# One chained attention–mixer–FNet kernel on Trainium2: thinner widening behind the last projection, slots opened inside channel block 0, slabs copied from SBUF

## The chip, the cores and the metric

The kernel runs on one core of a Trainium2 chip. The metric is the device time of one execution in microseconds. Of the kernel before three runs are shown; their median is 944.74 us, and they lie between 943.64 and 945.34.

## The reference: what is computed

Three layers follow one another on an activation of 4 × 576 tokens by 512 channels.

```python
def attention(q, k, v, omega):                    # 4 x 8 heads x 576 x 64, 128 features
    def phi(x):
        h = einsum('bhsd,md->bhsm', x, omega) - sum(x * x, -1) / 2
        return exp(h - max(h, -1)) / sqrt(m)
    q_p, k_p = phi(q * scale), phi(k * scale)
    kv, z = einsum('bhsm,bhsd->bhmd', k_p, v), sum(k_p, 2)
    return einsum('bhsm,bhmd->bhsd', q_p, kv) / (einsum('bhsm,bhm->bhs', q_p, z) + 1e-06)

def mixer(x, w_tok1, w_tok2, w_ch1, w_ch2):       # 576 -> 256 -> 576, 512 -> 1536 -> 512
    u = x + (relu(x.T @ w_tok1) @ w_tok2).T
    return u + relu(u @ w_ch1) @ w_ch2

def fourier(x, w_ch1, w_ch2):                     # 512 -> 2048 -> 512
    u = x + real(fft(fft(x, axis=1), axis=2))
    un = (u - mean(u)) / sqrt(var(u) + 1e-06)
    return u + relu(un @ w_ch1) @ w_ch2
```

The activations are float32; the weights of the two MLPs arrive as 64-bit floats.

## The kernel before

**Products.** Every operand of a product is split into a high and a low part of float32, and a product is three products on TensorE (PE): high by high, low by high, high by low. A channel MLP step takes one of twelve weight slabs (128 hidden units of `w_ch1` and `w_ch2`, high and low, 1 MB): `up` (L777) makes 12 matmuls into an H bank of PSUM, `relu` takes the high part on ACT (`hh`, L864) and the low part on DVE (`hl`, L865), and `down` (L902) makes 12 matmuls into four A banks that collect over all twelve slabs. `mlp` (L868) writes them in this order: up(i), relu(i), down(i−1), then a piece of other work. The tokens are cut into five blocks of 512 (the last has 256), in the order 0, 4, 1, 2, 3; every second block takes the slabs in reverse order.

**Widening.** The 64-bit weights are turned into pairs of float32 on the core (`widen`, L325 to L375), a chunk of 128 × 1024 words at a time. A chunk is loaded into `stg`, goes through seven DVE steps (take L342, rest L353, size L357, high L361, low L365, unit L369, scaled L373; ACT scales once in between), and its result in `cvo` is stored to DRAM as `kept` by `store` (L407 for a slab). There are two buffers each of `stg`, `cvy` and `cvo`, used in turn, so chunk i+2 writes its `cvo` where chunk i's was. `weave` (L384) strings the steps of neighbouring chunks together: four chunks of the token weights, the twelve slabs 0 to 11, then sixteen chunks for the last layer, which the prediction counts on from 12. `Side` (L200) gives them out: each slot of the attention and each step of an MLP adds an allowance in us to a credit, and steps are issued while the credit covers their cost. The allowances are a row of constants (L37):

```python
SLOT0_US, SLOT1_US, SLOT_US, FIRST_US, SHORT_US, CH_US, FF_US, S_US, SAVED_US = 1.2, 0.45, 1.2, 3.9, 1.2, 4.3, 3.8, 1.6, 4.6
side.step(0.0 if n < 6 else SLOT0_US if n < 10 else SLOT1_US if n < 36 else SLOT_US)
```

**Slots.** `Slots` (L258) keeps slabs in SBUF. `refill` goes through the sequence of slabs to come; for the first that isn't there it takes a free slot, or the one whose slab is needed latest, and fetches the slab from `kept` on SP's queue (`fetch`, L733). It stops at a slab that has not been stored yet. Two slots (`wa`) are there from the last projection on, three (`wb`) from attention's end, and five more (`wc`, `wd`) from the end of channel block 0. From attention's end on the widening's loads and stores go by POOL's queue (`side.queue`), fetches stay on SP's. A slot holds 1 MB.

**Attention's end.** `attention()` runs over slots n; the projections end at slot `n_all`, and seven slots follow in which the last `numer` (L583), `divide` (DVE L596, L599), transposes (`turn_x`, L617) and the first `up` of channel block 0 are written. The token mixing of the last quarter of the tokens (`tok_mix`) is cut into pieces in the list `fill`: two `hid` (L668) and eight `back` (six matmuls at L681, then a DVE add into `x2` at L684). A piece is taken per slot, and in channel block 0 one per step; what is left is written ahead of the last step's split. Token products take their bank by `bank`: while the list `spare` is not empty, they go around its banks (A, A, H), otherwise they have two S banks of their own. `spare` is emptied after attention.

**Tables.** `tables()` (L943, L944) loads two tables for the Fourier transform, by SP's and POOL's queues, ahead of the second channel block; `dft` first reads them in the fourth.

Of the kernel before, what the change touches and what calls it, by code (L numbers as in the profile page):

```python
# [28 lines left out]
NWB = 3  # L29
IDLE = 16  # L30
# [6 lines left out]
SLOT0_US, SLOT1_US, SLOT_US, FIRST_US, SHORT_US, CH_US, FF_US, S_US, SAVED_US = 1.2, 0.45, 1.2, 3.9, 1.2, 4.3, 3.8, 1.6, 4.6  # L37
# [220 lines left out]
class Slots:  # L258
# [3 lines left out]
    def __init__(self, seq, fetch, ready, wait):  # L262
        self.seq, self.fetch, self.ready, self.wait = seq, fetch, ready, wait
        self.free, self.here, self.at = [], {}, 0
        self.allow = lambda q, slot: True

    def refill(self, need=None):
        for q in range(self.at, len(self.seq)):
# [35 lines left out]
def mix_kernel(ctx: ExitStack, tc: tile.TileContext, qt, kt, va, om, w1, w2, wch, wff, t1, t2, out):  # L304
# [96 lines left out]
    kept = {}  # L401
    whole = set()

    def slab(j):
        def store(st, free):
            kept[j] = dram.tile([128, 2, 1024], F32, name="kept")
            side.queue.dma_start(out=kept[j], in_=st["o"].bitcast(F32))  # L407
            whole.add(j)
            free()
# [323 lines left out]
    def fetch(x, pl_, tag):  # L733
# [3 lines left out]
        else:  # L737
            t = pl_.tile([128, 2, 1024], F32R, tag=tag, name="w")
            sync.dma_start(out=t.bitcast(F32), in_=kept[x])
        return t  # L740

    def wait_whole(x):
# [5 lines left out]
                fetch, lambda x: x in whole, wait_whole)  # L748
    mix.allow = lambda q, slot: q < len(mix.seq) - 2 or slot[1] in ("wa0", "wa1", "wd")
# [32 lines left out]
    def attention():  # L782
# [35 lines left out]
        for n in range(-1, n_all + LAG_X):  # L818
            while loads and at[loads[0]] <= n + AHEAD_LOAD:
                load(*loads.pop(0))  # L820
            if n == n_all:
                enter_mlp()
            if 0 <= n < n_all:
# [8 lines left out]
            if n >= 2:  # L832

                side.step(0.0 if n < 6 else SLOT0_US if n < 10 else SLOT1_US if n < 36 else SLOT_US)
# [19 lines left out]
    side.defer, side.queue = 0, pool  # L854

# [12 lines left out]
    def mlp(steps, first_of, u, cols, down, budget, prepare, twice=False):  # L868
# [3 lines left out]
        for i, x in enumerate(steps):  # L872
# [11 lines left out]
            if not last:  # L884
                if fill:
                    fill.pop(0)()
# [5 lines left out]
    def ch_block(at_, c, u, prepare, budget):  # L892
# [12 lines left out]
        mlp(turns(NCH, at_), ch_first, u, cols, down, budget, prepare)  # L905
# [7 lines left out]
    def mixed():  # L913
        while fill:
            fill.pop(0)()

    ch_block(0, 0, u, [lambda: (mixed(), ch_split(BLOCKS[1], u2))], FIRST_US)
    u = u2
    pt.close()
    xu = ctx.enter_context(tc.tile_pool(name="xu", bufs=1, side="right", reuse_waits="tile"))  # L920
    c2 = ctx.enter_context(tc.tile_pool(name="c2", bufs=1, side="right", reuse_waits="tile"))

    pw = ExitStack()
    wc = pw.enter_context(tc.tile_pool(name="wc", bufs=1, side="right", reuse_waits="tile"))
    mix.free.extend((wc, f"wc{i}") for i in range(4))
# [676 lines left out]
```

## Time and profile before

| | |
|---|---|
| median of three runs | 944.74 us (943.64 to 945.34) |
| the profiled execution, its own time | 942.83 us |
| its span in the profile | 940.6 us |
| granted TensorE clock | 1.00 |
| PE busy | 930.3 us, 99% |
| DVE busy | 633.4 us, 67% |
| ACT, POOL busy | 305.7 and 118.9 us |
| DMA | 216.5 MB, mean 230 GB/s |
| chain that ended last | PE 92%, DVE 5%, DMA 1%, ACT 1% |

Between the profiled execution's time and its span lie 2.2 us around the program. The engines run side by side; a busy share near 100% names the engine that sets the time, and the idle time before its instructions, with what released each, says what could still be won. The chain that ended last is followed back from the last instruction; it lies on PE nearly throughout.

### The profile page before, as it was taken

The numbers are of one execution on the slowest core, as the hardware profiler recorded it, in microseconds if no ns is written. First come the engines' busy times: TensorE is split into PE (matmuls) and PEld (weight loads), VectorE is DVE, ScalarE is ACT, GpSimd is POOL, SyncE is SP. The second block draws the span as 40 slices with busy tenths as digits, with TensorE's granted clock in tenths as the row PEclk, the third lists the DMA queues.
The fourth block names the chain that finished last, engine by engine and source line by source line (L and its number), as shares of the span: only waits on it lengthen the run. The fifth ranks groups of instructions, "written<-read, shape, count | busy, mean of one in ns | idle before, by whom it ended". The sixth has DMA issues, their size and how long they took to land.

```text
span 940.6 us, 14116 instructions
## 1 busy us (share of the span) xinstructions
PE 930.3 (99%) x5360; PEld 830.1 (88%) x5360; DVE 633.4 (67%) x1259; ACT 305.7 (32%) x709; POOL 118.9 (13%) x110
## 2 busy tenths in 40 slices
PE   9999999989999999999999999999999999999998
PEld 8999999978889888888888888889999998899986
DVE  5987999896775778777853667766565457533342
ACT  5986777722121322122121122222311113211121
POOL 3453444221211122011000000000000000000000
PEclk9999999999999999999999999999999999999999
DMA  8765554687897586573245368739766656687764
GB/s 275 237 212 183 182 214 153 257 301 286 327 419 306 201 319 220 187 277 126 90 175 195 124 207 267 240 106 400 257 232 230 221 191 230 231 263 251 247 214 153
DMA packets 68258, 216.48 MB, mean 230 GB/s; under 512 B 5600, under 2 KB 14432, under 8 KB 54240
## 3 DMA queue, kind: packets, MB, share of 16 engines
q1 hardware_dynamic: 60992, 172.40, 52.5%
q0 software_dynamic: 7056, 43.06, 12.4%
q8 instruction: 43, 0.70, 0.3%
q14 instruction: 23, 0.19, 0.1%
q10 hardware_dynamic: 144, 0.13, 0.0%
HBM read 169.30 MB, written 42.47 MB: 225 GB/s over the span
## 4 chain that ended last, share of the span: by engine, by line
PE 92%; DVE 5%; DMA 1%; ACT 1%; issue 0%; POOL 0%; DVEq 0%; SPq 0%; ACTq 0%
PE H L777 23%; PE A L902 16%; PE A L1474 14%; PE H L1461 12%; PE A L1268 7%; PE A L507 4%; PE N L583 3%; PE H L541 2%; PE A L668 1%; PE A L566 1%; PE S L1081 1%; PE S L1094 1%; PE S L681 1%; PE H L668 1%; PE A L681 1%; PE S L668 1%
## 5 line engine op out<-in xcount | busy, mean ns | idle before, releaser
L777 PE MATMUL H<-uh,w 128*128 128x512 f32 (+1 forms) x800 | 215.2, 354 | 2.1 <-DVE x L684 2.1
L777 PEld LDWEIGHTS H<-uh,w 128*128 128x128 f32 x800 | 136.4, 189 | 22.3 <-DVE x L684 2.3
L864 ACT ACTIVATE hh<-H 128x512 fp32r<-128x512 f32 (+1 forms) x92 | 49.0, 533 | 270.4 <-PE H L777 270.2
L777 PE MATMUL H<-ul,w 128*128 128x512 f32 (+1 forms) x304 | 113.5, 373 | 0.4 <-DVE ul L764 0.4
L902 PE MATMUL A<-hh,w 128*128 128x512 f32 (+1 forms) x480 | 108.7, 369 | 0.0
L865 DVE SCALAR_TENSOR_TENSOR hl<-H,hh 128x512 fp32r<-128x512 f32 (+1 forms) x92 | 55.7, 606 | 65.5 <-ACT hh L864 65.3
L1474 PE MATMUL A<-w2t,b 128*128 128x512 f32 x384 | 99.2, 394 | 0.0
L902 PEld LDWEIGHTS A<-hh,w 128*128 128x128 f32 x480 | 84.2, 188 | 15.0
L1461 PE MATMUL H<-b,w1t 128*128 128x384 f32 x480 | 91.5, 336 | 0.0
L1461 PEld LDWEIGHTS H<-b,w1t 128*128 128x128 f32 x480 | 85.0, 188 | 4.0 <-DVE tmp L1505 0.3
L1474 PEld LDWEIGHTS A<-w2t,b 128*128 128x128 f32 x384 | 70.6, 188 | 11.8
L525 ACT ACTIVATE f<-A,mx 128x128 f32<-128x128 f32 x240 | 69.5, 396 | 22.9 <-DVE mx L521 22.5
L777 PEld LDWEIGHTS H<-ul,w 128*128 128x128 f32 x304 | 57.3, 189 | 9.9 <-DVE ul L764 0.8
L902 PE MATMUL A<-hl,w 128*128 128x512 f32 (+1 forms) x240 | 59.2, 368 | 0.0
L1268 PE MATMUL A<-w,hh 128*128 128x512 f32 x192 | 50.5, 395 | 0.0
L902 PEld LDWEIGHTS A<-hl,w 128*128 128x128 f32 x240 | 42.6, 188 | 7.6
L521 DVE TENSOR_REDUCE mx<-A 128x4 f32<-128x512 f32 x70 | 47.4, 680 | 1.7 <-PE A L507 1.4
L541 PE MATMUL H<-v,f 128*128 128x65 f32 x320 | 40.1, 270 | 0.5 <-ACT f L525 0.4
L1466 ACT ACTIVATE b<-tmp 128x384 fp32r<-128x384 f32 x16 | 8.4, 525 | 98.1 <-DVE tmp L1527 98.1
L361 DVE SCALAR_TENSOR_TENSOR cvo<-cvy,cvo 128x1024 int32<-128x1024 int32 (+2 forms) x32 | 39.7, 1240 | 0.5
L1268 PEld LDWEIGHTS A<-w,hh 128*128 128x128 f32 x192 | 34.6, 189 | 6.1
L541 PEld LDWEIGHTS H<-v,f 128*128 128x128 f32 x320 | 38.9, 191 | 0.9 <-ACT f L525 0.7
(263 smaller groups left out, 1687.5 us busy)
## 6 DMA issues: line engine op xcount, KB each, us to landing
w<-kept SPq DMA_DIRECT2D x60, 1024.0 KB, 6.9
w2t<-kept SPq DMA_DIRECT2D x55, 512.0 KB, 4.9
w1t<-kept SPq DMA_DIRECT2D x48, 512.0 KB, 5.1
stg<-in_wff_dram POOLq DMA_DIRECT2D x16, 1024.0 KB, 6.6
kept<-cvo POOLq DMA_DIRECT2D x13, 1024.0 KB, 7.2
stg<-in_wch_dram SPq DMA_DIRECT2D x9, 1024.0 KB, 6.2
kept<-cvo POOLq DMA_DIRECT2D x16, 512.0 KB, 7.4
kept<-so SPq DMA_DIRECT2D x16, 512.0 KB, 8.0
```

The source lines that it names most:

```text
L361: dve.scalar_tensor_tensor(out=st["h"], in0=st["y"].bitcast(I32), scalar=-0x80000000, in1=st["h"], op0=ALU.bitwise_and, op1=ALU.bitwise_or)
L507: pe.matmul(out=pj[:, p_ * 256:p_ * 256 + 256], lhsT=a[:, c, :], rhs=w, start=(n == 0), stop=(n == 2), skip_group_check=True)
L521: dve.tensor_reduce(out=mx, in_=p4, axis=AX.X, op=ALU.max, negate=True)
L525: act.activation(out=f[:, hh], in_=p4[:, hh], func=AF.Exp, bias=mx[:, hh])
L541: pe.matmul(out=kvp[b, g][:, hh * 65:hh * 65 + 65], lhsT=ft["k", i, g][:, hh, :], rhs=src["v", i, int(off > 0)][:, 4 * g + hh, :], start=( ...
L777: pe.matmul(out=hb[:, 0:n], lhsT=w(a, kk), rhs=u[:, kk, 0:n], start=(c == 0), stop=(c == 11))
L864: act.activation(out=hh, in_=hb[:, 0:n], func=AF.Relu)
L865: dve.scalar_tensor_tensor(out=hl, in0=hb[:, 0:n], scalar=0.0, in1=hh, op0=ALU.max, op1=ALU.subtract)
L902: pe.matmul(out=acc[i][:, 0:cols], lhsT=a[:, cs], rhs=v, start=(n == 0 and c_ == 0), stop=(n == NCH - 1 and c_ == 2))
L1268: pe.matmul(out=acc[t], lhsT=a[:, t * 128:t * 128 + 128], rhs=w, start=(n == 0 and c_ == 0), stop=(n == NFF - 1 and c_ == 2))
L1461: pe.matmul(out=to, lhsT=w[:, a, cs], rhs=v[:, q], start=(start and n == 0), stop=(n == 5), skip_group_check=True)
L1474: pe.matmul(out=acc[t], lhsT=h[n // 2][:, t * 128:t * 128 + 128], rhs=w[:, n % 2], start=(begins and n == 0), stop=(ends and n == 2))
```

## The change

Seven edits, in the order of the diff:

- `LOOK`: `refill` looks six slabs ahead of the step at work, not to the end of the sequence.
- `FIRST_US`, the widening's allowance a step in channel block 0, goes from 3.9 to 4.4.
- *Copies* (`direct`): from attention's end on, when a slab's widening is done, it is first offered to `refill`; if that takes it, it is copied from `cvo` to its slot in SBUF on POOL's queue, and the store to `kept` is issued behind the copy.
- `spare` is emptied when the last projection's slots begin (`n == n_all`).
- The seven slots behind the last projection get an allowance of 0.45 (`SLOT1_US`) and no longer 1.2.
- In channel block 0 two pieces of `fill` are written per step; as soon as the list is empty, the token mixing's tiles are given up and the five slots `wc` and `wd` opened (`filled`), which was done behind the block.
- `tables()` is called ahead of the third channel block and no longer ahead of the second.

```diff
@@ -27,6 +27,7 @@
 BLK = 512
 
 NWB = 3
+LOOK = 6
 IDLE = 16
 NBLK = (NTOK + BLK - 1) // BLK
 
@@ -34,7 +35,7 @@
 
 
 
-SLOT0_US, SLOT1_US, SLOT_US, FIRST_US, SHORT_US, CH_US, FF_US, S_US, SAVED_US = 1.2, 0.45, 1.2, 3.9, 1.2, 4.3, 3.8, 1.6, 4.6
+SLOT0_US, SLOT1_US, SLOT_US, FIRST_US, SHORT_US, CH_US, FF_US, S_US, SAVED_US = 1.2, 0.45, 1.2, 4.4, 1.2, 4.3, 3.8, 1.6, 4.6
 
 
 NP = NFF // 2
@@ -261,11 +262,11 @@
 
     def __init__(self, seq, fetch, ready, wait):
         self.seq, self.fetch, self.ready, self.wait = seq, fetch, ready, wait
-        self.free, self.here, self.at = [], {}, 0
+        self.free, self.here, self.at, self.ahead = [], {}, 0, len(seq)
         self.allow = lambda q, slot: True
 
     def refill(self, need=None):
-        for q in range(self.at, len(self.seq)):
+        for q in range(self.at, min(self.at + self.ahead, len(self.seq))):
             s = self.seq[q]
             if s in self.here:
                 continue
@@ -398,12 +399,17 @@
         return items
 
 
-    kept = {}
+    kept, fresh = {}, {}
     whole = set()
 
     def slab(j):
         def store(st, free):
             kept[j] = dram.tile([128, 2, 1024], F32, name="kept")
+            if mlp0.get("direct"):
+                fresh[j] = st["o"]
+                whole.add(j)
+                mix.refill()
+                del fresh[j]
             side.queue.dma_start(out=kept[j], in_=st["o"].bitcast(F32))
             whole.add(j)
             free()
@@ -736,7 +742,10 @@
             sync.dma_start(out=t.bitcast(F32), in_=kept[x][:, 0:4])
         else:
             t = pl_.tile([128, 2, 1024], F32R, tag=tag, name="w")
-            sync.dma_start(out=t.bitcast(F32), in_=kept[x])
+            if x in fresh:
+                side.queue.dma_start(out=t.bitcast(F32), in_=fresh[x].bitcast(F32))
+            else:
+                sync.dma_start(out=t.bitcast(F32), in_=kept[x])
         return t
 
     def wait_whole(x):
@@ -746,6 +755,7 @@
     mix = Slots([j for c in range(NBLK) for j in turns(NCH, c)]
                 + [(k, p_) for c in range(len(PLAIN)) for p_ in turns(NP, c) for k in (1, 2)],
                 fetch, lambda x: x in whole, wait_whole)
+    mix.ahead = LOOK
     mix.allow = lambda q, slot: q < len(mix.seq) - 2 or slot[1] in ("wa0", "wa1", "wd")
 
     def halves(t, h):
@@ -820,6 +830,7 @@
                 load(*loads.pop(0))
             if n == n_all:
                 enter_mlp()
+                spare.clear()
             if 0 <= n < n_all:
                 project(*order[n])
             sums(n)
@@ -831,7 +842,7 @@
             results(n)
             if n >= 2:
 
-                side.step(0.0 if n < 6 else SLOT0_US if n < 10 else SLOT1_US if n < 36 else SLOT_US)
+                side.step(0.0 if n < 6 else SLOT0_US if n < 10 else SLOT1_US if n < 36 or n >= n_all else SLOT_US)
             if fill and (len(fill) > 3 or n % 2 == 0):
                 fill.pop(0)()
             for fn in early[:3]:
@@ -852,6 +863,7 @@
     pools["S"] = ctx.enter_context(tc.tile_pool(name="ps_s", bufs=2, space=PSUM, reuse_waits="tile")), 2
 
     side.defer, side.queue = 0, pool
+    mlp0["direct"] = True
 
 
     hp = pm.enter_context(tc.tile_pool(name="hp", bufs=2, reuse_waits="tile"))
@@ -865,7 +877,7 @@
         dve.scalar_tensor_tensor(out=hl, in0=hb[:, 0:n], scalar=0.0, in1=hh, op0=ALU.max, op1=ALU.subtract)
         return hh, hl
 
-    def mlp(steps, first_of, u, cols, down, budget, prepare, twice=False):
+    def mlp(steps, first_of, u, cols, down, budget, prepare, twice=False, filled=None):
 
 
         prev = None
@@ -882,14 +894,18 @@
                 down(*prev)
             prev = i, x, h
             if not last:
-                if fill:
-                    fill.pop(0)()
+                for fn in fill[:2]:
+                    fn()
+                del fill[:2]
+                if filled and not fill:
+                    filled()
+                    filled = None
                 side.step(budget / 2 if twice else budget)
         for fn in prepare[1:]:
             fn()
         down(*prev)
 
-    def ch_block(at_, c, u, prepare, budget):
+    def ch_block(at_, c, u, prepare, budget, filled=None):
         acc = [bank("A") for _ in range(4)]
         cols = ch_cols(c)
 
@@ -902,7 +918,7 @@
                     pe.matmul(out=acc[i][:, 0:cols], lhsT=a[:, cs], rhs=v, start=(n == 0 and c_ == 0),
                               stop=(n == NCH - 1 and c_ == 2))
             mix.used()
-        mlp(turns(NCH, at_), ch_first, u, cols, down, budget, prepare)
+        mlp(turns(NCH, at_), ch_first, u, cols, down, budget, prepare, filled=filled)
         for i in range(4):
             for off, n, b, s in pieces(c * BLK, cols):
                 dve.tensor_tensor(out=x2[b][:, i, s:s + n], in0=acc[i][:, off:off + n], in1=x2[b][:, i, s:s + n],
@@ -910,21 +926,20 @@
 
     u = mlp0["u"]
     u2 = operand()
-    def mixed():
-        while fill:
-            fill.pop(0)()
-
-    ch_block(0, 0, u, [lambda: (mixed(), ch_split(BLOCKS[1], u2))], FIRST_US)
+    rooms = {}
+
+    def filled():
+        pt.close()
+        rooms["xu"] = ctx.enter_context(tc.tile_pool(name="xu", bufs=1, side="right", reuse_waits="tile"))
+        rooms["c2"] = ctx.enter_context(tc.tile_pool(name="c2", bufs=1, side="right", reuse_waits="tile"))
+        rooms["wc"] = pw.enter_context(tc.tile_pool(name="wc", bufs=1, side="right", reuse_waits="tile"))
+        mix.free.extend((rooms["wc"], f"wc{i}") for i in range(4))
+        mix.free.append((pm.enter_context(tc.tile_pool(name="wd", bufs=1, reuse_waits="tile")), "wd"))
+
+    pw = ExitStack()
+    ch_block(0, 0, u, [lambda: ch_split(BLOCKS[1], u2)], FIRST_US, filled)
     u = u2
-    pt.close()
-    xu = ctx.enter_context(tc.tile_pool(name="xu", bufs=1, side="right", reuse_waits="tile"))
-    c2 = ctx.enter_context(tc.tile_pool(name="c2", bufs=1, side="right", reuse_waits="tile"))
-
-    pw = ExitStack()
-    wc = pw.enter_context(tc.tile_pool(name="wc", bufs=1, side="right", reuse_waits="tile"))
-    mix.free.extend((wc, f"wc{i}") for i in range(4))
-    wd = pm.enter_context(tc.tile_pool(name="wd", bufs=1, reuse_waits="tile"))
-    mix.free.append((wd, "wd"))
+    xu, c2, wc = (rooms[name] for name in ("xu", "c2", "wc"))
 
     def leave_slots():
         mix.leave(wc)
@@ -1380,9 +1395,10 @@
     def temps():
         return [tmp[k][:, i] for k in range(2) for i in range(2)]
 
-    tables()
     for at_ in range(1, NBLK):
 
+        if at_ == 2:
+            tables()
         if at_ == 3:
             leave_slots()
             f2 = ctx.enter_context(tc.tile_pool(name="f2", bufs=1, side="right", reuse_waits="tile"))
```

**PE at attention's end.** In the tile names of what follows the number is the buffer's: `N` is the bank of the last transposes, `x` and `h1h`, `h1l` are the token mixing's activations, `uh` is the channel block's operand. The program's order on PE before, from the last transposes to the second `up` of channel block 0:

```order
L617 MATMUL N_2894<-ident_66,x_2840 128x128 [waits DVE_49,PE_49]
L617 MATMUL N_2894<-ident_66,x_2840 128x128 x3
L681 MATMUL H_2901<-w2hl_100,h1h_2622 128x288 x2
L681 MATMUL H_2901<-w2hl_100,h1l_2623 128x288
...
L681 MATMUL S_2930<-w2hl_100,h1h_2622 128x288 x2
L681 MATMUL S_2930<-w2hl_100,h1l_2623 128x288
...
L777 MATMUL H_2942<-uh_2706,w_2747 128x512 [waits DMAHW5_49,DVE_49]
```

And the same place after:

```order
L623 MATMUL N_2886<-ident_66,x_2837 128x128 [waits DVE_49,PE_49]
L623 MATMUL N_2886<-ident_66,x_2837 128x128 x3
L687 MATMUL A_2892<-w2hl_100,h1h_2622 128x288 x2
L687 MATMUL A_2892<-w2hl_100,h1l_2623 128x288
...
L687 MATMUL S_2921<-w2hl_100,h1h_2622 128x288 x2
L687 MATMUL S_2921<-w2hl_100,h1l_2623 128x288
...
L687 MATMUL S_2929<-w2hl_100,h1h_2622 128x288 [waits Activation_49]
...
L687 MATMUL S_2929<-w2hl_100,h1l_2623 128x288
...
L787 MATMUL H_2945<-uh_2706,w_2746 128x512 [waits DMAHW5_49]
```

The last token product of attention has moved from an H bank to an A bank, a second product stands ahead of the second `up`, and that `up` no longer waits for DVE.

**DVE in the late steps of channel block 0.** `stg`, `cvy` and `cvo` are the widening's buffers; `hl` is the low half of a step's relu. Before, from slab 11's scaled to the chunk behind the next (chunks 12 and 13):

```order
L373 SCALAR_TENSOR_TENSOR cvo_3159<-cvo_3159,cvy_3158 128x1024 [waits DVE_49]
L353 TENSOR_SCALAR cvo_3212<-stg_3161 128x1024 [waits DMASW7_49]
...
L865 SCALAR_TENSOR_TENSOR hl_3276<-H_3262,hh_3275 128x512 [waits Activation_49]
L684 TENSOR_TENSOR x2_2596<-S_3293,x2_2596 128x288 [waits PE_49]
...
L373 SCALAR_TENSOR_TENSOR cvo_3212<-cvo_3212,cvy_3211 128x1024 [waits DVE_49]
L865 SCALAR_TENSOR_TENSOR hl_3326<-H_3312,hh_3325 128x512 [waits Activation_49]
L684 TENSOR_TENSOR x2_2596<-S_3341,x2_2596 128x288 [waits PE_49]
L353 TENSOR_SCALAR cvo_3304<-stg_3214 128x1024 [waits DMASW1_49]
```

After, from slab 10's scaled (`cvo_3138`) to the `hl` of step 8 (`hl_3361`); `DMASW` are the semaphores of POOL's queue:

```order
L374 SCALAR_TENSOR_TENSOR cvo_3138<-cvo_3138,cvy_3137 128x1024 [waits DVE_49]
L354 TENSOR_SCALAR cvo_3260<-stg_3140 128x1024 [waits DMASW5_49]
L877 SCALAR_TENSOR_TENSOR hl_3284<-H_3270,hh_3283 128x512 [waits Activation_49]
...
L877 SCALAR_TENSOR_TENSOR hl_3323<-H_3309,hh_3322 128x512 [waits Activation_49]
L374 SCALAR_TENSOR_TENSOR cvo_3260<-cvo_3260,cvy_3259 128x1024 [waits DVE_49]
L354 TENSOR_SCALAR cvo_3305<-stg_3262 128x1024 [waits DMASW7_49,DMASW0_49]
L358 TENSOR_SCALAR cvo_3305<-cvy_3304 128x1024 [waits Activation_49]
L362 SCALAR_TENSOR_TENSOR cvo_3305<-cvy_3304,cvo_3305 128x1024 [waits DVE_49]
L877 SCALAR_TENSOR_TENSOR hl_3361<-H_3347,hh_3360 128x512 [waits Activation_49]
```

The token adds (L684, now L690) no longer stand between these steps, and chunk 12's rest now waits for two transfers of POOL's queue (slab 10's copy and its store) with an `hl` behind it.

**The queues.** Fetches on SP, from the last slab that is fetched in channel block 0 on; `kept_3257` before is slab 11; after, `kept_3191` is slab 9, and `kept_2451`, `kept_2226`, `kept_2016`, `kept_1811` and `kept_1575` are slabs 4, 3, 2, 1 and 0. Before:

```order
L739 DMA w_3291<-kept_3257 128x2048 [waits DMAHW4_49,DMASW1_49,PE_49]
L943 DMA t1_sb_3523<-in_t1_dram 128x647
L739 DMA w_3584<-kept_2878 128x2048 [waits Pool_49]
L739 DMA w_3586<-kept_2675 128x2048
L739 DMA w_3588<-kept_2451 128x2048 [waits DMAHW5_49]
L739 DMA w_3590<-kept_2226 128x2048 [waits DMAHW6_49]
```

After:

```order
L748 DMA w_3225<-kept_3191 128x2048 [waits DMAHW2_49,DMASW5_49,PE_49]
L748 DMA w_3606<-kept_2451 128x2048
L748 DMA w_3642<-kept_2226 128x2048
L748 DMA w_3675<-kept_2016 128x2048 [waits Pool_49]
L748 DMA w_3707<-kept_1811 128x2048 [waits DMAHW3_49,DMASW2_49,PE_49]
L748 DMA w_3739<-kept_1575 128x2048 [waits DMAHW4_49,DMASW7_49,PE_49]
L958 DMA t1_sb_3516<-in_t1_dram 128x647 [waits DMAHW5_49]
```

And POOL's queue after, from chunk 12's load (`stg_3262`) to chunk 14's; `cvo_3138` is slab 10, `cvo_3260` slab 11:

```order
L332 DMA stg_3262<-in_wff_dram 128x2048 [waits DMASW2_49,DVE_49]
L746 DMA w_3266<-cvo_3138 128x2048 [waits DVE_49,PE_49,Pool_49]
L413 DMA kept_3265<-cvo_3138 128x2048
L332 DMA stg_3307<-in_wff_dram 128x2048 [waits DMASW4_49,DMASW1_49,DVE_49]
L746 DMA w_3341<-cvo_3260 128x2048 [waits DVE_49,PE_49]
L413 DMA kept_3340<-cvo_3260 128x2048 [waits DMASW3_49]
L332 DMA stg_3381<-in_wff_dram 128x2048 [waits DMASW6_49,DVE_49]
```

Slabs 10 and 11 are copied (`w<-cvo`) and then stored; SP fetches slabs of the next block behind slab 9, and the tables stand behind all of these.

## Rows read from the trace of the kernel before

**Rows 1.** The page: span; busy time, share of the span and instructions by engine.

```profile
span 940.6 us, 14116 instructions
...
PE 930.3 (99%) x5360; PEld 830.1 (88%) x5360; DVE 633.4 (67%) x1259; ACT 305.7 (32%) x709; POOL 118.9 (13%) x110
```

**Rows 2.** Waits of PE, whole span: us in total, times, longest us.

```profile
PE H L777 <- DVE x L684: 2.1, 1, 2.1
...
PE N L617 <- DVE x L599: 1.0, 1, 1.0
...
PE H L777 <- DVE ul L764: 0.4, 1, 0.4
```

**Rows 3.** Timeline of PE, 192 to 207 us: start, us, line, op, [idle before].

```profile
193.56 1.00 PE L583 MATMUL N<-kvs,qpT 128*128 128x65 f32 x8
...
196.41 0.63 PE L617 MATMUL N<-ident,x 128*128 128x128 f32 x4 [1.00 <-DVE x L599]
...
198.34 0.29 PE L681 MATMUL S<-w2hl,h1l 128*128 128x288 f32 x1
200.73 0.50 PE L777 MATMUL H<-uh,w 128*128 128x512 f32 x1 [2.09 <-DVE x L684]
...
203.58 1.98 PE L902 MATMUL A<-hh,w 128*128 128x512 f32 x8
205.39 1.07 PE L902 MATMUL A<-hl,w 128*128 128x512 f32 x4
```

**Rows 4.** Timeline of DVE, 190 to 205 us.

```profile
193.87 1.22 DVE L365 SCALAR_TENSOR_TENSOR cvo<-cvo,stg 128x1024 f32<-128x1024 int32 x1
...
195.37 0.15 DVE L596 TENSOR_SCALAR rd<-N 128x4 f32<-128x4 f32 x1
...
195.77 0.49 DVE L599 TENSOR_TENSOR x<-N,rd 128x128 f32<-128x128 f32 x2
...
200.23 0.44 DVE L684 TENSOR_TENSOR x<-H,x 128x288 f32<-128x288 f32 x1
```

**Rows 5.** Chain that ended last, 190 to 232 us: start, us, engine, tile, line.

```profile
206.46 0.79 PE S L681 x6
...
212.71 3.46 PE S L668 x15
216.17 2.76 PE H L777 x12
218.93 2.72 PE A L902 x12
```

**Rows 6.** Timeline of DVE, 230 to 250 us.

```profile
233.00 1.22 DVE L373 SCALAR_TENSOR_TENSOR cvo<-cvo,cvy 128x1024 fp32r<-128x1024 f32 x1
...
245.42 0.69 DVE L353 TENSOR_SCALAR cvo<-stg 128x1024 int32<-128x1024 int32 x1
...
246.74 1.23 DVE L361 SCALAR_TENSOR_TENSOR cvo<-cvy,cvo 128x1024 int32<-128x1024 int32 x1
247.88 0.68 DVE L865 SCALAR_TENSOR_TENSOR hl<-H,hh 128x512 fp32r<-128x512 f32 x1
```

**Rows 7.** Stretches 206 to 218 and 254 to 289 us: last columns clock, DMA share, GB/s.

```profile
206.00:218.00 12.00, 12.00 (x57) 9.98 (x56) 6.39 (x9) 2.26 (x3) 1.03 (x1) 1.00 0.91 345
254.00:289.00 35.00, 35.00 (x210) 31.41 (x210) 25.10 (x39) 7.08 (x14) 5.46 (x8) 1.00 1.00 405
```

**Rows 8.** DMA queues, 254 to 289 us: kind, packets, MB, share of 16 engines.

```profile
q1 hardware_dynamic: 1107, 7.43, 51.9%
q0 software_dynamic: 1099, 6.71, 48.0%
```

**Rows 9.** DMA issues, 206 to 254 us: count, KB each, median us to landing.

```profile
kept<-cvo POOLq DMA_DIRECT2D x4, 1024.0 KB, 7.6
```

**Rows 10.** DMA issues, whole span: count, KB each, median us to landing.

```profile
kept<-cvo SPq DMA_DIRECT2D x7, 1024.0 KB, 5.3
...
w1hl<-cvo SPq DMA_DIRECT2D x2, 640.0 KB, 5.2
```

## The prediction, made before the changed kernel ran

> **What bounds the kernel now.** I read the page's busy line first, then the waits of PE, then the timelines around the longest of them. TensorE is busy for 930.3 of 940.6 us [rows 1], so an edit of order can only win what PE idles, or lose by making it idle. PE's waits inside the program are few [rows 2]: 2.1 us for a DVE add into `x2` (L684), 1.0 us for the last `divide` (L599), 0.4 us for an operand split (L764). All three lie in attention's tail, between 189 and 201 us. [Rows 3] show the larger two: the last transposes start at 196.41 after 1.00 us of idle time, the second `up` at 200.73 after 2.09. [Rows 4] show why. DVE is behind: it runs a widening step at 193.87, so the last `divide` begins only at 195.37, although its product, begun at 193.56, ended at 194.56 [rows 3]; and the add that frees the H bank runs at 200.23, although the bank's product was done before 198. In channel block 0 behind it PE never waits, and that is where the change puts work back.
>
> **Names.** A slab's chunk is widened in seven DVE steps: take, rest, size, high, low, unit, scaled. Chunks 0 to 11 are `wch` slabs, 12 and up come from `wff`. `hl(i)` is the DVE half of the relu of block 0's step i.
>
> **The tail (gain).** Over the seven slots behind the last projection the allowance falls from 1.2 to 0.45 us a slot. The step at 193.87 becomes a rest of 0.69 instead of a low of 1.22, and two long steps ahead of it leave, so DVE is free when the product ends; the last `divide` begins at 194.6 instead of 195.37. PE's 1.00 falls to 0.2: **0.8 us**. With `spare` cleared early, the second `up` takes an H bank that no token product has just used, so the 2.09 goes: **2.1 us**. What is late next: the four A banks of the first `down`, whose adds now run before its start, 2.7 us after the `up`'s. The 0.4 stays: that split waits for ACT, whose queue ahead of it is unchanged. Sum −2.9.
>
> **Block 0 (cost).** PE's work is the same: an `up` or a `down` 2.72, a token back product 0.79, a hidden one 3.46 [rows 5]. With two of `fill` a step and no wait, the second `up` starts at 196.41 − 0.8 + 2.06 (to the end of the S product, [rows 3]) + 0.79 = 198.45; step 1 takes 5.44 + 6.92, steps 2 to 5 7.02 each, the rest 5.44. So up(6) starts at 238.9, up(9) at 255.2, up(10) at 260.7, up(11) at 266.1. DVE is behind the back products of step 5 until 239.4; low, unit, take and scaled of slab 10 end at 242.9. Scaled of slab 11 ends at 249.9, and rest of chunk 12 is due at once, 7.0 us after slab 10's scaled.
>
> That rest overwrites the `cvo` buffer of slab 10, so it waits for every DMA that reads it. In before that is one store: scaled began at 233.00, rest at 245.42 [rows 6], and a store takes 7.6 [rows 9], some 3.6 us of slack. Now it is a copy to the slot and a store behind it, on one queue, and DVE holds `hl(8)` behind the rest. In the same time SP has slab 9's fetch (its store: 233.5 + 7.6 = 241.2) and, because the new slots are already free, three fetches of the next block's slabs right behind. From 241.2 there are thus four MB on SP's queue and six on POOL's (load 12, copy and store of 10, load 13, copy and store of 11). Saturated, the DMA engines moved 405 GB/s [rows 7], in halves for the two queues [rows 8]: 1.05 MB each way in 5.2 us. Slab 10's store is the third of POOL's six: 256.8. From rest's start to the end of the `hl` behind it takes 245.42 to 248.56, so 3.1 [rows 6]: 259.9. PE wants `hl(8)` at 255.2 + 2.72 + 1.81 (eight `hh` matmuls, [rows 3]) = 259.7, so 0.2 late. Slab 11's store ends the ten: 10.5 MB / 405 = 25.9 us, 267.1. Rest of chunk 13 waits for it and `hl(9)` follows, 0.69 + 0.68 [rows 6]: 268.5. PE wants it at 260.7 + 2.72 + 1.81 = 265.2: **3.3 us late** (the 0.2 is in it). Four steps and an `hl` more per step follow; `hl(10)` holds, `hl(11)`, whose `down` follows the one before without an `up` between, is by the same count about **0.6** late. Sum +3.9.
>
> The nearest rows bound this cost. Below: if POOL's queue is served at once, slab 11's copy lands as a lone store does now and its store one transfer behind, 249.9 + 7.6 + 2.6 (1.05 MB at 405 GB/s) = 260.1; `hl(9)` ends at 261.5, before PE's 265.2, and the cost is nothing. Above: the copy stays inside SBUF, and such copies of 640 KB took 5.2 us where a 1,024 KB store took 5.3 [rows 10]; at 1.6 times the price a byte, each of two copies costs 0.6 × 2.6 us more, 3.1 in all, and the cost is 7.0. I take 3.9, since rows 7 are a saturated stage of the same two queues.
>
> The Trainium skill (DMA: Bandwidth & Descriptors, Specifications) gives a ceiling of 435 GB/s instead of the 405 of rows 7; by it the ten transfers end at 265.3, the cost is 2.1 and the sum −0.8. No stretch here holds that rate, so the row decides.
>
> **Edits at nothing.** `FIRST_US` 4.4 gives eleven steps 0.5 us more, 5.5 in all, against 7 × 0.75 = 5.25 taken from the tail, so the widening is level at the block's end and PE has 5.44 a step over it. The tables leave the stage of rows 7 for the next block; their reader comes two blocks later. The short block fetches five slabs instead of seven, three of them early, so its cover grows. At the fourth block two slabs that lay in the given-up slots are fetched again; both queue behind the block before, a block's length ahead of use. If that cover were gone, one fetch would show, about 7 us.
>
> **Sum.** −2.9 + 3.9 = +1.0. On the profiled execution that is 942.8 + 1.0 = 943.8; the median of the runs shown is 1.9 above that execution, and the forecast stands on the median: **945.7 us**. Its own range, with the cost between 1.5 and 6, is 943.3 to 947.8. A difference under 0.2% (1.9 us, so 942.9 to 946.6 is no change) can't be told from none.
>
> **Rivals.**
> *The copies are in time.* If POOL's queue is served ahead of SP's, the lower bound above holds, `hl(9)` ends 3.7 us before PE wants it, no PE wait appears and the tail's gain stays: 944.7 − 2.9 = 941.8. For it: before has no wait in block 0 at all, and PE's needs are a block away for SP's three fetches. Against: [rows 8], where neither queue went ahead of the other. Chance 0.30.
> The Trainium skill (DMA: Bandwidth & Descriptors, Issuing engines are not separate DMA queues) says that issuing from several engines only saves issue time; by it the copies on POOL's queue take from SP's fetches, and the halves of rows 8 agree.
> *Copies in SBUF are dear* (slower). If a copy inside SBUF costs 1.6 times a store's byte, as rows 10 may say, slab 11's store ends 3.1 us later, at 270.2, and each 1 us of that is 1 us of `hl(9)`: 945.7 + 3.1 = 948.8. It decides from a copy price of about 1.25 on. For it: rows 10. Against: those copies stood among small loads. Chance 0.14.
> *The tail's wait only changes its name* (slower): the first `down` waits for A banks that DVE has not emptied, so the 2.1 stays and block 0 costs as above: 945.7 + 2.1 = 947.8. It holds if DVE is still over 2.7 us behind at 198.5. Against: it has 5 us less to do. Chance 0.08.
>
> **How the numbers follow.** My forecast has 0.48. Faster by over 0.2%: the first rival and the forecast's lowest end, 0.31. Slower: the last two, and the forecast's upper third, 0.28. No change: 0.41. The range takes in the first rival and the second, each widened by what the runs shown lie from their median, 1.1 below and 0.6 above: 940.7 to 949.4.
>
> **What would show it.** Right: PE's waits at L684 and L599 near 200 us gone or under 0.3; a new PE wait of 2 to 4 us for `hl` between 255 and 275; DVE waiting for DMA at the rest step (L354) twice, for 4 us or more; DMA share near 1.00 from 241 to 267. Wrong: no such PE wait, or a wait for `w`, or any wait behind 290 us.

## The result, and the profile after

The changed kernel takes 948.84 us (median of 6 runs, 946.54 to 951.51), the kernel before beside it 944.27 (6 runs, 943.00 to 945.34): a ratio of 1.0055, with a 95% interval of 1.0042 to 1.0067. It is **slower by 4.6 us**. The profiled execution of after took 951.51 us, the slowest of its six, with a span of 949.5, so its rows show more than the usual loss: 8.9 us of span, where the medians differ by 4.6.

The page of after, against [rows 1]:

```profile
span 949.5 us, 14127 instructions
...
PE 933.8 (98%) x5360; PEld 831.8 (88%) x5360; DVE 633.8 (67%) x1259; ACT 306.2 (32%) x709; POOL 118.7 (13%) x112
```

PE does the same 5360 matmuls, but is busy for 3.5 us more: some of them ran slower. The waits of PE in after, against [rows 2] (us in total, times, longest):

```profile
PE A L918 <- DVE hl L877: 7.0, 2, 4.7
...
PE H L787 <- DVE ul L774: 0.4, 1, 0.4
...
PE N L623 <- DVE x L605: 0.2, 1, 0.2
```

The wait for the add (2.1) is gone and that for the last `divide` (1.0) is 0.2; in their place PE waits 7.0 us for `hl`, twice. The timeline of PE in after shows where (start, us, line, op, [idle before]), against [rows 3]:

```profile
188.86 0.39 PE L787 MATMUL H<-uh,w 128*128 128x512 f32 x1
...
196.47 0.63 PE L623 MATMUL N<-ident,x 128*128 128x128 f32 x4 [0.24 <-DVE x L605]
...
199.33 0.39 PE L787 MATMUL H<-uh,w 128*128 128x512 f32 x1
...
263.35 1.20 PE L918 MATMUL A<-hl,w 128*128 128x512 f32 x4 [2.30 <-DVE hl L877]
...
273.86 2.07 PE L918 MATMUL A<-hl,w 128*128 128x512 f32 x4 [4.70 <-DVE hl L877]
...
280.16 2.03 PE L918 MATMUL A<-hh,w 128*128 128x512 f32 x8
...
285.76 0.28 PE L787 MATMUL H<-uh,w 128*128 128x256 f32 x1
```

The first row is the first `up` of channel block 0, the last row the first `up` of the second block. From one to the other takes 96.90 us; in before it is 187.97 to 277.66, 89.69. So 7.2 of the 8.9 us lie here; 0.9 lie ahead of the first row and 0.8 behind the last. Behind the second wait four matmuls of 512 columns take 2.07 us, where they took 1.07 in [rows 3]: the granted clock is lower there, as the last window below shows. The timeline of DVE shows what `hl` waited for, against [rows 6]:

```profile
242.90 1.22 DVE L374 SCALAR_TENSOR_TENSOR cvo<-cvo,cvy 128x1024 fp32r<-128x1024 f32 x1
...
250.04 1.21 DVE L374 SCALAR_TENSOR_TENSOR cvo<-cvo,cvy 128x1024 fp32r<-128x1024 f32 x1
260.13 0.69 DVE L354 TENSOR_SCALAR cvo<-stg 128x1024 int32<-128x1024 int32 x1 [8.88 <-DMA kept<-cvo]
...
262.61 0.68 DVE L877 SCALAR_TENSOR_TENSOR hl<-H,hh 128x512 fp32r<-128x512 f32 x1
...
267.16 1.22 DVE L374 SCALAR_TENSOR_TENSOR cvo<-cvo,cvy 128x1024 fp32r<-128x1024 f32 x1
272.51 0.69 DVE L354 TENSOR_SCALAR cvo<-stg 128x1024 int32<-128x1024 int32 x1 [4.13 <-DMA kept<-cvo]
273.12 0.68 DVE L877 SCALAR_TENSOR_TENSOR hl<-H,hh 128x512 fp32r<-128x512 f32 x1
```

Slab 10's scaled ends at 244.1 and slab 11's at 251.2; the rest steps of chunks 12 and 13 (L354) then wait 8.88 and 4.13 us for the stores of these slabs, and behind each of them stands an `hl`. The same stretch by windows of after (the last columns are PEclk, DMA share and GB/s):

```profile
240.00:243.00 3.00, 3.00 (x16) 2.45 (x15) 2.81 (x5) 0.05 (x1) 0.93 (x1) 1.00 0.06 27
243.46:246.00 2.54, 2.54 (x13) 2.11 (x12) 2.50 (x5) 1.04 (x2) 1.29 (x2) 1.00 0.81 258
246.00:250.00 4.00, 4.00 (x19) 3.31 (x18) 4.00 (x5) 1.04 (x2) 1.07 (x2) 1.00 0.99 317
250.00:264.70 14.70, 12.40 (x55) 9.97 (x54) 5.79 (x8) 1.82 (x3) 1.06 (x2) 1.00 1.01 424
264.70:272.41 7.71, 4.46 (x20) 3.29 (x18) 2.15 (x3) 1.55 (x2) 2.06 (x3) 1.00 1.02 426
243.46:272.41 28.95, 23.40 (x102) 18.68 (x100) 14.44 (x18) 5.44 (x8) 5.47 (x8) 1.00 0.99 395
...
272.50:279.30 6.80, 5.45 (x13) 4.29 (x14) 6.76 (x9) 1.06 (x1) 1.03 (x1) 0.50 0.49 181
```

From 246 to 272.4 the DMA engines are full (shares of 0.99 to 1.02). From 272.5 to 279.3 the granted clock is 0.50, which is 1.2 GHz. That is not the profiled execution's alone: the mean granted clock of the six runs of after is 0.996 to 0.998, and 0.996 in the profiled one. The DMA issues of 244 to 273 us in after are these (count, KB each, median us to landing):

```profile
w<-kept SPq DMA_DIRECT2D x3, 1024.0 KB, 19.1
w<-cvo POOLq DMA_DIRECT2D x2, 1024.0 KB, 14.3
kept<-cvo POOLq DMA_DIRECT2D x2, 1024.0 KB, 17.5
```

By these medians the three early fetches of the next block, the two copies and the two stores take 1.9 to 2.5 times the 7.6 us of a store in [rows 9]. The store ahead of them, slab 9's (issues of 234 to 236 us), was late already:

```profile
kept<-cvo POOLq DMA_DIRECT2D x1, 1024.0 KB, 8.4
```

### The profile page after: what moved, and what is told of

It reads as the page before. It is cut to its first block, busy times and chain, and to the rows that moved or that the text cites. A ratio compares the mean times of both kernels' runs of the same rounds, so it can differ in the third digit from the quotient of the medians.

```text
span 949.5 us, 14127 instructions
## 1 busy us (share of the span) xinstructions
PE 933.8 (98%) x5360; PEld 831.8 (88%) x5360; DVE 633.8 (67%) x1259; ACT 306.2 (32%) x709; POOL 118.7 (13%) x112
## 4 chain that ended last, share of the span: by engine, by line
PE 90%; DVE 5%; DMA 3%; ACT 1%; issue 1%; DVEq 0%; POOL 0%; SPq 0%; ACTq 0%; POOLq 0%
PE H L787 21%; PE A L918 14%; PE A L1490 14%; PE H L1477 12%; PE A L1283 7%; PE A L513 4%; PE N L589 3%; PE H L547 3%; DMA kept<-cvo 2%; PE A L674 1%; PE A L572 1%; PE S L1096 1%; PE A L687 1%; PE S L1109 1%; PE S L687 1%; PE H L674 1%
## 5 line engine op out<-in xcount | busy, mean ns | idle before, releaser
L876 ACT ACTIVATE hh<-H 128x512 fp32r<-128x512 f32 (+1 forms) x92 | 49.1, 533 | 270.3 <-PE H L787 270.2
L350 ACT ACTIVATE cvy<-cvy 128x1024 f32<-128x1024 f32 (+2 forms) x32 | 32.8, 1026 | 26.5 <-DVE cvy L343 26.4
```

Of the source, the lines that this page charges most:

```text
L876: act.activation(out=hh, in_=hb[:, 0:n], func=AF.Relu)
```

## The experiments

The theory after this: **the three early fetches** fill the DMA engines just when slabs 10 and 11 are stored, DVE's rest step waits for the stores and holds `hl`, and the clock falls behind the longer wait. The rivals: the copies themselves are too much; the higher allowance brings the rest step ahead of `hl`; the tail's time has to be paid back in any case. The column "block 0" is the stretch measured above, read in each profile from the same two instructions. The ratio comes from all runs of a version, the last two columns from the one execution of it that was profiled.

| run | ratio to before (95%) | block 0, us | PE waits in it behind the tail |
|---|---|---|---|
| before | 1 | 89.69 | none |
| after | 1.0055 (1.0042 to 1.0067) | 96.90 | hl 2.30, 4.70 |
| no early fetch | 0.9980 (0.9965 to 0.9995) | 87.35 | hl 0.2 |
| two early fetches | 1.0026 (1.0015 to 1.0037) | 90.40 | hl 1.36, 0.98, 0.34 |
| no copies | 1.0030 (1.0020 to 1.0039) | 91.74 | w 1.13, hl 2.86 |
| tail alone | 0.9990 (0.9976 to 1.0004) | 88.26 | w 1.44 |
| lower allowance | 1.0010 (0.9997 to 1.0023) | 93.31 | hl 3.43 |
| late fetch, 3.9 | 0.9960 (0.9947 to 0.9972) | 86.87 | none |
| late fetch, 3.9, no copies | 1.0031 (1.0013 to 1.0050) | 93.51 | w 4.24 |
| busy wait, half | 1.0083 (1.0050 to 1.0115) | 95.65 | hl 1.15, 2.34 |
| busy wait, whole | 1.0058 (1.0038 to 1.0078) | 94.86 | hl 0.30, 0.17, 0.32 |

### No early fetch

`first` ends `refill`'s look at block 0's last slab; behind the block the fetches are issued by POOL's queue, because on SP's queue nothing would hold them back: in the order after the change two of the three stand there without a wait.

```diff
-        for q in range(self.at, min(self.at + self.ahead, len(self.seq))):
+        for q in range(self.at, min(self.at + self.ahead, self.first)):
...
+    mix.ahead, mix.first = LOOK, NCH
...
+                queue = side.queue if x in (2, 3, 4) and NCH <= mix.at < 2 * NCH else sync
...
+    mix.ahead, mix.first = 10, len(mix.seq)
+    mix.refill()
+    mix.ahead = LOOK
```

> The changed kernel, but slabs 4, 3 and 2 of the next block are fetched only behind channel block 0 (on POOL's queue); the copies, the early slots and the thinner tail stay. Theory (SP's three early fetches share the DMA engines with slab 10's and 11's copies and stores, so DVE's rest step waits and holds the hl behind it): from 243.5 to slab 11's store there are seven MB and not ten, 7.3 / 0.42 = 17.5 us, so that store lands near 261 instead of 272.4 and PE wants hl(9) at 266.7. Both PE waits for hl (2.3 and 4.7 us) go, the granted clock stays 1.00, and the tail's gain is left: 2.9 us faster than before, near 941.4. Rival (the copies alone are too much for POOL's queue): the two waits stay, at 4 us or more, and the time stays 2 us or more above before.

Measured: 941.33 us (10 runs) against 943.47 of before (31 runs), 2.1 us faster where 2.9 were expected. The waits of PE, then of DVE from 240 to 275 us:

```profile
PE A L919 <- DVE hl L878: 0.2, 1, 0.2
```

```profile
DVE cvo L354 <- DMA kept<-cvo: 5.7, 2, 3.9
```

The 7.0 us fall to 0.2. DVE still waits 5.7 us for the stores, but no longer into the time when PE wants `hl`. The copies are as in after, so by themselves they are not the cause. This profiled execution had a lower clock early in the attention (0.74 between 20 and 40 us), where the kernels are alike; its block 0 stands beside that.

### Two early fetches

The same edit with `first` at `NCH + 9`: slabs 4 and 3 are fetched early, slab 2 behind the block.

> The changed kernel, but only slabs 4 and 3 are fetched early, slab 2 behind the block. Theory: one MB less ahead of slab 11's store is 1.05 / 0.42 = 2.5 us, so PE's wait for hl(9) falls from 4.7 to about 2.2; slab 10's store lands before slab 2's share begins, so the wait for hl(8) stays near 2.3. The clock does not fall behind so short a wait (it stayed at 1.00 behind the 2.3). Against before: -2.9 + 2.3 + 2.2 = 1.6 us slower, about 945.9. Rival (the copies alone): as the changed kernel, 4.5 us slower than before.

Measured: 945.43 us, by the ratio of 1.0026 2.4 us slower than before. The timeline of PE has three waits and no lower clock behind them:

```profile
261.48 1.20 PE L919 MATMUL A<-hl,w 128*128 128x512 f32 x4 [1.36 <-DVE hl L878]
...
268.28 1.19 PE L919 MATMUL A<-hl,w 128*128 128x512 f32 x4 [0.98 <-DVE hl L878]
...
277.28 1.20 PE L919 MATMUL A<-hl,w 128*128 128x512 f32 x4 [0.34 <-DVE hl L878]
```

2.7 us in all, between 7.0 with three early fetches and 0.2 with none, and the ratios stand in the same order: 1.0055, 1.0026, 0.9980. The dose tells: it is the fetches. By how much one fetch counts, these waits don't tell, because the burst began earlier here. Slab 9's store, for which SP's fetches wait, landed in 5.7 us and not in 8.4 (DMA issues of 233.5 to 236 us). Counted from the first `up` of block 0, slab 9's fetch was issued at 51.9 us (239.83 − 187.92), in after at 54.6 and without early fetches at 54.2; so those two can be compared as they stand. The profiled execution also has the lowest time of the ten (943.78 us). In the five from 945.62 us on the granted clock is 0.996 to 0.998, so there the clock fell too. That the first wait would stay at 2.3 was wrong, it fell to 1.36; in after slab 2's fetch was issued at 245.0, ahead of slab 10's store (245.2, 14.9 us to landing), so it shared in that store.

### No copies

```diff
-    mlp0["direct"] = True
```

> The changed kernel without the copies: slabs 10 and 11 are stored and then fetched by SP, as before the change. The early fetches then stand on SP's queue behind slab 11's fetch and so behind its store. Theory: neither the copies nor the early fetches are in the stage, slab 10's store lands near 252 and slab 11's near 260, no wait for hl; slab 11's fetch lands near 266 where its up is due at 267, so 0 to 1 us of waiting for w. 2 to 2.9 us faster than before: 941.4 to 942.3. Rival (the higher allowance brings the rest step ahead of hl, whatever the DMAs do): waits for hl of 3 us or more stay.

Measured: 946.11 us, ratio 1.0030. The forecast missed: it did not become faster than before. The timelines of PE and DVE:

```profile
268.19 0.50 PE L787 MATMUL H<-uh,w 128*128 128x512 f32 x1 [1.13 <-DMA w<-kept]
...
278.78 1.21 PE L917 MATMUL A<-hl,w 128*128 128x512 f32 x4 [2.86 <-DVE hl L876]
```

```profile
275.57 0.69 DVE L354 TENSOR_SCALAR cvo<-stg 128x1024 int32<-128x1024 int32 x1 [5.14 <-DMA kept<-cvo]
```

Without the copies the early fetches stand on SP's queue behind slab 11's fetch and start only at 259, and there they meet the next store, chunk 12's; chunk 14's rest waits 5.14 us for it with the last `hl` behind. So the burst costs here too, though later, and slab 11's own fetch is 1.13 us late besides. The wait of 2.86 is near the 3 of the rival, but DVE's row shows the DMA that held the rest step.

### The tail alone

The kernel before with `FIRST_US` 4.4, `spare.clear()` at the last projection, and the thinner tail:

```diff
-                side.step(0.0 if n < 6 else SLOT0_US if n < 10 else SLOT1_US if n < 36 else SLOT_US)
+                side.step(0.0 if n < 6 else SLOT0_US if n < 10 else SLOT1_US if n < 36 or n >= n_all else SLOT_US)
```

> The kernel before with three edits alone: the allowance of 0.45 behind the last projection, spare emptied at the last projection, and 4.4 a step in channel block 0. Theory (the tail's gain is a matter of its own): PE's waits of 2.09 and 1.00 near 200 us fall to 0.3 or less, nothing new in block 0: 2.9 us faster than before, 941.4. Rival (the higher allowance in block 0 costs something itself): waits for hl or w of 1 us or more between 240 and 280.

Measured: 942.68 us, ratio 0.9990, not clear of 1; 2.9 us were expected. The waits near 200 us are gone, but PE has a new one:

```profile
PE H L777 <- DMA w<-kept: 1.4, 1, 1.4
```

It is the `up` of slab 11. The tail's widening, given up, makes the last slab late; with 1.44 us there, block 0 gains 1.43 us instead of 2.9. The wait is one that the rival named, but the higher allowance can hardly be its cause: without the copies it was 1.13 us at 4.4 and, in the last version below, 4.24 at 3.9.

### Lower allowance

The changed kernel with `FIRST_US` back at 3.9.

> The changed kernel with the allowance in channel block 0 back at 3.9; copies, early slots and early fetches stay. Slab 10's scaled then stands behind the hl of step 6, and chunk 13's rest ahead of the hl of step 10 instead of step 9. Theory (what a rest step costs is set by which hl stands behind it on DVE): slab 10's store lands about 1.5 us later, but size and high no longer lie between chunk 12's rest and hl(8), so that wait stays near 2; slab 11's store lands near 274, and hl(10) is wanted at 272 to 274, so 1 to 2 us there and none at hl(9). 3 to 4 us of waits and not 7.0, no lower clock: 0 to 1 us slower than before. Rival (the order on DVE is of no account, the DMAs alone set it): 7 us of waits, 4.6 us slower.

Measured: 944.33 us, ratio 1.0010, where 0 to 1 us slower was expected. The waits are half those of after, in one place (timeline of PE):

```profile
263.17 2.07 PE L918 MATMUL A<-hl,w 128*128 128x512 f32 x4 [3.43 <-DVE hl L877]
```

That it fell on one `hl`, and that the clock fell behind it, was not expected. The place of the rest step on DVE counts too: slab 11's store lands at 269.2 (13.2 us from 256.0), and `hl(9)`, now ahead of the rest step that waits for it, has run at 266.6. How much of the 3.6 us is the order's is open, because here too slab 9's store landed early, in 5.4 us, and the burst began 2.4 us earlier than in after, counted from the first `up`.

### Late fetch and 3.9: the version that beats both

"No early fetch" with `FIRST_US` at 3.9.

> The next block's slabs fetched behind channel block 0 (as in the run without early fetches) and the allowance there at 3.9. Theory: no PE wait for hl at all (0.2 us is left without this edit), the tail's gain remains, the widening is some 5 us later and nobody waits for that: 2 to 3 us faster than before, 940.5 to 941.5, faster than both kernels. Rival (the tail's time must be paid back in this block): a wait for w or for the widening of 2 us or more in a later block, and no gain.

Measured: **940.04 us** (5 runs, 938.68 to 940.39) against 943.29 (15 runs): ratio 0.9960, faster than both kernels. PE waits for nothing from 200 us to the end of block 0. The waits of DVE from 240 to 275 us, and the DMA issues of 238 to 268:

```profile
DVE cvo L354 <- DMA kept<-cvo: 1.3, 2, 0.7
```

```profile
w<-cvo POOLq DMA_DIRECT2D x2, 1024.0 KB, 5.4
kept<-cvo POOLq DMA_DIRECT2D x2, 1024.0 KB, 7.5
```

A copy inside SBUF lands in 5.4 us and the store behind it in 7.5. Block 0 takes 86.87 us, 2.82 less than before: that is the tail's gain without a loss. The ratio shows somewhat more (3.8 us). Of the 3.7 us of span between the two profiled executions 1.0 lies ahead of the first `up` (186.95 beside 187.97), a place that differs by up to 1.9 us between these profiles. Of the 15 runs of before beside it, 5 had a granted clock of 0.998, and three of these had the longest times of all; of these five runs none was below 0.999. Where in before the clock falls can't be seen, since its profiled execution had 1.00.

### Late fetch and 3.9, without the copies

The last version without `mlp0["direct"] = True`.

> The version with late fetches and the allowance at 3.9, without the copies: slabs 10 and 11 are stored and then fetched by SP. Theory (the copies cost nothing and buy little once the early fetches are gone): slab 11's store, issued where its copy was (251.9), lands near 258, its fetch near 264.5, and its up is due at 265.3; 0 to 1 us of waiting for w, no wait for hl: 2.5 to 3.6 us faster than before. Rival (the copies are what a tail thinned by 5 us needs): slab 11 comes 2 us or more late and half of the gain is lost.

Measured: 946.09 us, ratio 1.0031: 2.9 us slower than before and not faster. The rival was right, and the loss is larger than it said:

```profile
270.21 0.79 PE L788 MATMUL H<-uh,w 128*128 128x512 f32 x1 [4.24 <-DMA w<-kept]
```

Slab 11 has to go out to DRAM and back, two transfers one after the other, and comes 4.24 us late; the clock falls as well (0.50 from 270.2 to 274.8 us). Against the version with copies this is 0.0071 of the ratio, some 6.7 us. The copies are what a tail with less widening needs; beside the early fetches they still left a loss.

### Busy waits

Does PE's lower clock cost something of its own? Transposes of the identity, thrown away, stand ahead of the `hl` products of steps 8 and 9 of the changed kernel (first 9 and 20 of them, then 18 and 40):

```diff
             for c_, (a, v) in enumerate(((hi, hh), (lo, hh), (hi, hl))):
+                if c_ == 2 and at_ == 0 and n in (8, 9):
+                    idle = bank("S")
+                    for _ in range(18 if n == 8 else 40):
+                        pe.transpose(idle[:, 0:128], ident, ident)
```

> The changed kernel, with work that is thrown away put on PE where it waits: 9 transposes of the identity ahead of the hl products of step 8, 20 ahead of those of step 9 of channel block 0 (16 of them took 3.67 us at the program's start, so about 2.1 and 4.6 us). Theory (the wait costs twice: 7.0 us of idle time, and the lower clock behind the 4.7, at which 5.8 us of work took some 2.6 us more): the waits are as long, but PE is busy in them, the granted clock stays at 1.00 behind 272, and the time is 2 to 3 us below the changed kernel's, about 2 us slower than before. Rival (the lower clock is an accident of the profiled run or comes whatever PE does): clock 0.996 again and the time as the changed kernel's, 4.6 us slower than before.

> The changed kernel with thrown-away transposes ahead of the hl products of step 8 (18) and step 9 (40) of channel block 0; in the run before this one 9 took 1.14 us and 20 took 2.35, half of what was assumed, so these take 2.3 and 4.7. Theory (the lower clock follows PE's idle time): PE idles less than 1 us in the two waits, the clock stays at 1.00 behind them, and from the first up to the end of the block the profile shows 97 - 2.7 = 94.3 us, where the changed kernel took 96.9 (5.4 us of its work ran at the lower clock). The time is some 2.7 us below the changed kernel's, about 2 us slower than before. Rival (the clock falls whatever PE does there): 96.9 again and clock 0.996.

In the first run the transposes took half of what was assumed, 1.14 and 2.35 us, and 1.15 and 2.34 us of waiting were left; its clock still fell, so it says little (timeline of PE):

```profile
272.60 2.07 PE L922 MATMUL A<-hl,w 128*128 128x512 f32 x4 [2.34 <-DVE hl L877]
```

In the second, by the timeline of PE and one window of it:

```profile
259.57 2.13 PE L919 MATMUL S<-ident 128*128 128x128 f32 x18
261.99 1.20 PE L922 MATMUL A<-hl,w 128*128 128x512 f32 x4 [0.30 <-DVE hl L877]
...
267.66 4.53 PE L919 MATMUL S<-ident 128*128 128x128 f32 x40
272.35 1.21 PE L922 MATMUL A<-hl,w 128*128 128x512 f32 x4 [0.17 <-DVE hl L877]
...
276.20 2.03 PE L922 MATMUL A<-hh,w 128*128 128x512 f32 x8
```

```profile
273.00:280.00 7.00, 7.00 (x32) 5.61 (x31) 6.97 (x9) 2.76 (x6) 2.06 (x2) 1.00 0.51 184
```

The `hl` comes as late as in after (within 0.2 us, counted from the first `up`), but PE is busy, the clock stays at 1.00, and the four `hl` matmuls behind the wait take 1.21 us instead of 2.07. From these four to the next `hh` matmuls it takes 3.85 us (272.35 to 276.20), in after 6.30 (273.86 to 280.16). Block 0 takes 94.86 us instead of 96.90, near the 94.3 expected: the lower clock had cost at least **2.0 us** in the profiled execution, 2.5 by the two stretches. In the time of the runs this doesn't show (948.69 in 4 runs, as against 948.84), and the forecast of some 2 us slower than before missed for both runs: by the ratios they are 7.8 and 5.5 us slower. The thrown-away work is a fixed 6.7 us, while after's waits may differ from run to run; its times do (946.54 to 951.51), its waits are known of one execution only. One of the four runs has a granted clock of 0.997 even so. What the clock costs in the median is left open.

## Why the prediction was right and wrong

**The tail: right.** −2.9 was forecast; block 0 of the version without waits is 2.82 shorter, and the last `divide`'s wait is 0.24 where 0.2 was said. What was missed is that this gain has a price of its own: without the copies the last slab comes late (1.44 and 4.24 us). The text let the widening be "level at the block's end" and did not ask about slab 11 on the way.

**Block 0: the mechanism was right, its size wrong.** The two rest steps, the DMAs that they wait for, and `hl(8)` and `hl(9)` behind them are in the trace as forecast. The step that failed is the cost term: it was 3.9 us and is 10.0 in the profiled execution (96.90 − 86.87); in the medians it is about 7.4, an estimate from the 4.6 us of loss and the 2.8 of gain. Three pieces of it were mis-sized. *The start:* slab 9's store was to land at 241.2; it was issued at 235.0, took 8.4 us and landed at 243.4, and that run was 0.9 us later from its start. The DMA share, which was to be near 1.00 from 241 on, is so from 246. *The bytes:* ten transfers, 10.5 MB, were counted to the end of slab 11's store. Chunk 12's stores and chunk 14's load are issued before that store lands, and the engines share: 11.4 MB went by between 243.46 and 272.41, at 395 GB/s. Later start 2.3, 0.9 MB more 2.4, rate 0.6: 5.3 us in all, which is what lies between 267.1 and 272.4. PE itself came 1.6 us later to `hl(9)` than forecast (273.86 − 4.70 − 2.30 = 266.86 beside 265.2), so the waits grew by 3.7, from 3.3 to 7.0. That is the upper bound of the text, by another way; the 0.6 for `hl(11)` did not come. *The clock:* there was no term for it; behind the 4.70 us of idle time PE ran at 0.50 for 6.8 us, some 2.5 us of loss. Waits and clock make 9.5 of the 10.0; the rest is not assigned.

The Trainium skill (TensorE: Matmul & The Clock Gate, Part 1) says that "the default state is throttled, and activity releases the throttle"; this case's trace agrees, with 0.50 behind the 4.70 us of idle time and 1.00 where the same wait was filled. The sum had no term for it.

The 435 GB/s of the Trainium skill (DMA: Bandwidth & Descriptors, Specifications), by which the cost would have been 2.1, are nearer to the full stretches here (424 and 426) than the 405 that I took. Yet the sum by it would have been further off: of the pieces that were wrong, rate was the smallest, 0.6 us.

**The rivals.** *Copies in time* fell: it needed POOL's queue to be served first, and copies and fetches took 14 and 19 us side by side. *Copies are dear* named a time, 948.8, that came out, for a reason that did not: without the early fetches a copy takes 5.4 us. That its time came out is luck. *The tail's wait only changes its name* fell: no wait for A banks.

**The chances.** Slower had 0.28, too little. Its own parts give more: the last two rivals have 0.22, and an upper third of the forecast's 0.48 is another 0.16, 0.38 in all. And the three mis-sized pieces all erred to the late side, so the upper bound of 7.0 deserved as much as the middle.

## What to carry to other kernels

Here a prefetch into slots that came free early was issued at once, though its reader was in the next block, and three of them cost 7.0 us of waits. Ask whose transfer a prefetch will share the DMA engines with, and put it on a queue behind that one when its reader can wait. When a step that waits for a DMA stands on its engine ahead of a step that TensorE needs, count the bytes that are issued up to the landing, not up to the issue (0.9 MB and 2.4 us here). A wait of some us on a full TensorE is to be costed with the slower matmuls that can follow it (2.5 us behind 4.70 here).

## What was not expected of the hardware

- **One engine's tail.** Between 240 and 243 us in after the DMA share is 0.06, as much as one engine of sixteen, at 27 GB/s (the first row of the windows above), while SP waits for slab 9's store; that store took 8.4 us, and 3 of them are this tail. In the profiles of the versions made from after the same store took 8.0 to 8.7 us (no early fetch, no copies, both busy waits) or 5.0 to 5.7 (two early fetches, and the three versions with the allowance of 3.9). What decides between the two no run shows. The Trainium skill (DMA: Bandwidth & Descriptors, Why a DMA increments its semaphore by 16 and not by 1) says that the engines of a transfer finish independently of each other; the row of 0.06 agrees.
- **The clock falls behind some short waits and not behind others.** It fell behind 3.43 us (lower allowance), 4.70 (after), 2.86 (no copies, 0.50 from 279.9 to 283.2 us) and even 2.34 (busy wait, half), and not behind the 2.30 of after: the length of the wait alone does not tell. Two windows around the 3.43:

```profile
258.00:262.00 4.00, 1.74 (x8) 1.12 (x6) 0.18 (x1) 0.60 (x1) 0.00 (x0) 1.00 1.01 424
262.00:269.00 7.00, 5.83 (x14) 4.58 (x15) 6.96 (x9) 0.77 (x1) 1.29 (x2) 0.52 0.87 330
```

- **A copy inside SBUF is not dearer than a store**, as far as two copies tell: 5.4 us a MB without the early fetches, where stores took 5.3 on SP's queue [rows 10] and 7.6 on POOL's [rows 9]. [Rows 10] had let one fear 1.6 times the price.
- **A transpose in a stream takes 0.11 us** (40 in 4.53), half of the 0.23 at the start of the program (16 in 3.67). The trace has no record of the clock so early (its first begins at 5.9 us in before), so whether it was the lower level there is not shown.

Not tried: the look of six slabs and the later tables by themselves. Both stay in the faster version.
